# First batch of an attention and gated feed-forward kernel: pooled products written four times into the banks of the banded ones

## The chip, the cores and the metric

The kernel runs on one core of a Trainium2 chip. The metric is the time of one execution on the device in microseconds (us), as the median of several runs. Engines are named as the profile names them: PE is TensorE (PEld its weight loads), DVE VectorE, ACT ScalarE, POOL GpSimd, SP SyncE, which issues the DMAs.

## The reference, cut to what matters

```python
q, k, v: (8, 8, 576, 64) float32; w_in: (512, 2048), w_out: (2048, 512)
# attention, per batch and head
q_d, k_d, v_d = means of four neighbouring rows of q, k, v
out_d   = softmax(q_d k_d^T / 8) v_d                 # 144 rows
mask    = |i - j| < 4
out_loc = softmax(where(mask, q k^T / 8, -1e9)) v    # 576 rows
x = repeat(out_d, 4 rows each) + out_loc             # -> (4608, 512)
# gated feed-forward
h = x @ w_in
out = (h * clip(h + 3, 0, 6) / 6) @ w_out
```

## The kernel before, in words

Work is planned as a list of operations with engines, costs and due times; `Plan.emit` orders them by list scheduling into one queue for each engine, and every queue runs strictly in that order. What an operation may wait for is therefore decided by its place in the queue and by its semaphores.

**Attention.** A unit is one batch and two heads (`plan_unit`, 4 units for each of 8 batches); two units are a duo (`plan_duo`). A unit computes the pooled products (rows of q and k summed in fours, `scores_d`, softmax, `trans_d`, `evict_d`, `pv_d`) and the banded ones (`scores`, ten windows of 64 rows, softmax, `trans`, `evict`, `pv`). v's rows are summed in fours by `sum4` (L361 to L370), by DVE or POOL. For the first batch (b = 0) and the second (`ALONE`) everything is turned by TensorE. `mean` (L551) scales the pooled result and takes it from PSUM to SBUF as `od`, and `add` (L614) adds `od`, each column four times, to the banded result in PSUM and writes x^T to SBUF: for the first batch as 288 + 224 columns in `x0` and 64 in `tail`.

**Feed-forward.** Tokens go in 12 parts (`PART`: 512, 256, then ten of 384). `plan_split` makes x^T's two parts (`hi`, a rounded copy, and `lo`, the rest). For each part and each of 16 blocks f of the hidden width, `gemm1` makes 12 matmuls (L860), `relu`, `gate`, `hi` and `lo` follow on ACT, DVE and POOL, and `gemm2` makes 3 matmuls for each 128 tokens (L910). `plan_store` evicts (L830, L832) and stores (L836).

**Weights.** They arrive as 64-bit floats, 512 KB a block, 32 blocks, and are made into two parts each by `plan_weight`: `rebias` and `low` on ACT (L172, L176, L190), `bits` twice on DVE (L181, L185), `hi` on ACT (L195), `lo` on DVE or POOL (L199).

`busy` (L943) fills expected gaps of TensorE with matmuls whose result nobody reads.

```python
nc.vector.tensor_tensor(x.rearrange("e (q r) -> e q r", r=4), px[...],
    od[:, lo // 4:hi // 4].unsqueeze(2).broadcast_to([P, (hi - lo) // 4, 4]), op=ALU.add)
```

Of the kernel before, what the change touches and what calls it, by code (L numbers as in the profile page):

```python
# [56 lines left out]
def tile_local_down_attention_moe(ctx, tc, q_all, k_all, v_all, _qk_loc, _v_loc, w_in, w_out, ident_d, _mask_d, out):  # L57
# [34 lines left out]
    def buf(key, holder, shape):  # L92
# [34 lines left out]
    head = const.tile([NAR, 2], F32, name="head")  # L127

# [23 lines left out]
    raw_t, zf_t, win, wout = {}, {}, {}, {}  # L152
    w_half, w_hi, w_done = {}, {}, {}

    def plan_weight(n, kind, f, after, gate):
        key = kind, f
        words = {}

        def load():
            raw_t[key] = wts.tile([P, 1024], I32, name=f"raw{kind}{f}", tag=f"w{kind}{f}")  # L160
            nc.sync.dma_start(raw_t[key], (w_in if kind == "i" else w_out)[f].bitcast(I32))
            w = raw_t[key].rearrange("p (n t) -> p n t", t=2)
            words["low"], words["high"] = w[:, :, 0], w[:, :, 1]

        by_bank = n < EARLY_BLOCKS and n % BY_BANK[1] < BY_BANK[0]
        zs = "zs0" if n < EARLY_Z[0] else "zs1" if n < EARLY_Z[1] else "zs"

        def rebias():

            if by_bank:  # L170
                zf_t[key] = bank(place[0], key)
                nc.scalar.activation(zf_t[key], words["high"].bitcast(F32), AF.Copy, scale=2.0 ** -112)  # L172
            else:
                zf_t[key] = buf(zs, key, [P, 512])
                high = words["high"].bitcast(F32)
                nc.scalar.activation(high, high, AF.Copy, scale=2.0 ** -112)  # L176

        def bits(i):
            z, high = zf_t[key].bitcast(I32), words["high"]
            if i == 0:  # L180
                nc.vector.scalar_tensor_tensor(  # L181
                    out=z, in0=z if by_bank else high, scalar=3, in1=words["low"],
                    op0=ALU.logical_shift_left, op1=ALU.bitwise_or)
            else:
                nc.vector.scalar_tensor_tensor(  # L185
                    out=z, in0=high, scalar=-0x80000000, in1=z, op0=ALU.bitwise_and, op1=ALU.bitwise_or)

        def low():

            nc.scalar.activation(words["low"], words["low"].bitcast(U32), AF.Copy, scale=2.0 ** -29, bias=-0.5)  # L190

        def hi():
            w = wts.tile([P, 2, 512], F32R, name=f"w{kind}{f}", tag=f"w{kind}{f}")
            (win if kind == "i" else wout)[f] = w
            nc.scalar.copy(w[:, 0], zf_t[key])  # L195

        def lo(eng):
            w = (win if kind == "i" else wout)[f]
            eng.tensor_tensor(w[:, 1], zf_t[key], w[:, 0].bitcast(F32), op=ALU.subtract)  # L199

        ld = op("SP", 0.5, load, list(after) + ([w_hi[gate]] if gate else []), size=dma(P, 4096))
        place = "zf0" if by_bank else zs, key
        a = op("ACT", 0.68, rebias, [ld], take=[place], lag=LAGW)
        c = op("ACT", 0.68, low, [ld], lag=LAGW)
        b = op("DVE", 0.75, partial(bits, 0), [a, c], lock=not by_bank)
        d = op("DVE", 0.75, partial(bits, 1), [b], lock=not by_bank)
        e = w_hi[key] = op("ACT", 0.6, hi, [d])
        if by_bank:
            w_done[key] = op("DVE", 0.72, partial(lo, nc.vector), [e], free=[place])
        else:  # L210
            w_done[key] = op(on("lo", 1.0), 0, lo, [e], free=[place], lock=True)


    xt = {}
# [72 lines left out]
    def plan_unit(b, d, u, row0, k0, kv, PS, duo, evicts, users, masked, early_user, due):  # L287
# [7 lines left out]


# [49 lines left out]
        def ld4(g):  # L346
            if b == 0 and "raw4" not in st:
                st["raw4"] = buf("raw4", ("v", un), [P, 2, 4, ROW])
            raw = st["raw4"][:, g] if b == 0 else buf("raw" + k0, ("v", un, g), [P, 4, ROW])
            if g == 0:  # L350
                nc.sync.dma_start(raw, src(v_all, row0, [[4 * ROW, P], [1, 4 * ROW]]))
            else:
                n = 1 if alone else 2
                raw = raw[:n * KR]
                for h in range(n):
                    nc.sync.dma_start(
                        raw[h * KR:(h + 1) * KR], src(v_all, row0 + 4 * P, [[4 * ROW, KR], [1, 4 * ROW]]))
            st["raw", g] = raw

        def sum4(g, eng):  # L360
            if "vd" not in st:  # L361
                st["vd"] = buf("vd" + k0, un, [P, 2, ROW])
            raw = st["raw", g]
# [6 lines left out]
            if g and not alone:  # L370
# [3 lines left out]
                eng.memset(st["vd"][NAR:D, 1], 0.0)  # L374

# [5 lines left out]
        for g in range(2):  # L381
            rk = ("raw4", ("v", un)) if b == 0 else ("raw" + k0, ("v", un, g))
            l = op("SP", 0.5, partial(ld4, g), take=[rk], size=dma((P, KR if alone else NAR)[g], 2048), nd=1 if alone else 1 + g)
            if b == 0:
                loads.append(l)
            sums.append(early_user(op(
                on("sum4", 1.0), 0, partial(sum4, g), [l], take=[("vd" + k0, un)], free=[rk])))
# [42 lines left out]
        def weigh(x, p, m, s):  # L430
# [5 lines left out]
            nc.scalar.activation(s, s, AF.Copy, bias=1e-9)  # L436
# [19 lines left out]
        def norm(eng, x, s):  # L456
            eng.tensor_tensor(x, x, s.unsqueeze(2).broadcast_to(list(x.shape)), op=ALU.mult)  # L457
# [952 lines left out]
```

## Time and profile before

| | |
|---|---|
| median of 3 runs | 957.76 us (956.91 to 960.08) |
| profiled execution, its own time | 956.95 us |
| its span, first to last instruction | 954.8 us |
| PE busy | 931.0 us, 98% of the span |
| DVE, ACT, POOL busy | 573.0, 368.2, 279.3 us |
| first matmul of the feed-forward starts at | 40.26 us |
| DMA | 93.53 MB, 98 GB/s in the mean |

How to read it: a share of busy time is a mean over stages. The feed-forward's matmuls of 10 of the 12 parts run back to back; what is not spent there lies in the first third and in the last microseconds. A matmul of float32 operands leaves two records in the trace (an operation of 4 matmuls is x8), a transpose and a matmul of the rounded type one.

### The profile page before, as it was taken

Reading aid. Unit: us, or ns where it says so; the run is one execution under the profiler, and the core shown is the slowest. Engines: PE = TensorE matmul, PEld = TensorE weight load, DVE = VectorE, ACT = ScalarE, POOL = GpSimd, SP = SyncE. Lnnn points to the kernel's source line nnn. Section 1 sums busy time; section 2 is a strip of 40 time slices with the busy share of each in tenths; the row PEclk is TensorE's granted clock in tenths of the full one; section 3 lists DMA queues with packets and bytes.
Section 4 is the critical chain, followed back from the end, with each engine's and each line's share of the span. In section 5 each row is a group of like instructions: output and inputs, shape, how many; then the busy total and the mean of one; then the engine's idle time right before and its main releaser. Section 6 shows DMA issues by size and latency. Waiting matters only on the chain.

```text
span 954.8 us, 19793 instructions
## 1 busy us (share of the span) xinstructions
PE 931.0 (98%) x7498; PEld 805.4 (84%) x7498; DVE 573.0 (60%) x1096; ACT 368.2 (39%) x915; POOL 279.3 (29%) x371
## 2 busy tenths in 40 slices
PE   7979999999999999999999999999999999999996
PEld 4667777888888888888988888888988888998995
DVE  6989887677656566657356667556656463222322
ACT  4787654434334324333233323423433332322321
POOL 5945434244434334323023342214113110000000
PEclk9999999999999999999999999999999999999999
DMA  7996435356665554555424464644514420100101
GB/s 213 265 307 128 126 107 102 81 113 131 120 130 113 118 112 97 102 87 112 94 62 83 102 117 83 128 90 99 117 27 92 94 61 1 34 1 1 34 1 33
DMA packets 311376, 93.53 MB, mean 98 GB/s; under 512 B 251377, under 2 KB 297329, under 8 KB 311281
## 3 DMA queue, kind: packets, MB, share of 16 engines
q1 hardware_dynamic: 311280, 92.27, 43.2%
q8 instruction: 59, 0.97, 0.4%
q14 instruction: 37, 0.29, 0.1%
HBM read 69.60 MB, written 22.61 MB: 97 GB/s over the span
## 4 chain that ended last, share of the span: by engine, by line
PE 88%; DMA 3%; SPq 2%; DVE 2%; POOL 2%; ACT 1%; issue 1%; DVEq 0%; POOLq 0%
PE h L860 40%; PE o L910 40%; PE a L612 2%; PE a L572 2%; PE a L413 1%; PE a L535 1%; PE a L910 1%; DMA early<-in_v_dram 1%; DMA rawo<-in_w_out_dram 1%; DMA rawi<-in_w_in_dram 1%; SPq L300 1%; POOL early L368 1%; SPq L252 0%; SPq L487 0%; DVE arena L870 0%
## 5 line engine op out<-in xcount | busy, mean ns | idle before, releaser
L860 PE MATMUL h<-rounded,wi 128*128 128x384 f32 (+2 forms) x2240 | 433.2, 336 | 5.0 <-ACT wi L195 3.7
L910 PE MATMUL o<-wo,rounded 128*128 128x512 f32 x1680 | 429.1, 396 | 1.0 <-POOL rounded L878 0.9
L860 PEld LDWEIGHTS h<-rounded,wi 128*128 128x128 f32 x2240 | 389.8, 188 | 28.5 <-ACT wi L195 4.5
L910 PEld LDWEIGHTS o<-wo,rounded 128*128 128x128 f32 x1680 | 308.1, 188 | 62.4 <-issue 4.6
L870 DVE SCALAR_TENSOR_TENSOR arena<-arena,h 128x384 f32<-128x384 f32 (+2 forms) x192 | 105.0, 547 | 175.0 <-ACT arena L866 174.5
L866 ACT ACTIVATE arena<-h 128x384 f32<-128x384 f32 (+2 forms) x192 | 94.1, 490 | 285.5 <-PE h L860 279.9
L874 ACT CAST rounded<-arena 128x384 fp32r<-128x384 f32 (+2 forms) x192 | 98.4, 513 | 145.9 <-DVE arena L870 107.8
L878 DVE TENSOR_TENSOR rounded<-arena,rounded 128x384 fp32r<-128x384 f32 (+2 forms) x154 | 87.1, 567 | 103.0 <-PE o L910 77.0
L878 POOL TENSOR_TENSOR rounded<-arena,rounded 128x384 fp32r<-128x384 f32 (+2 forms) x38 | 42.8, 1126 | 213.2 <-PE o L910 137.9
L442 POOL TENSOR_TENSOR arena<-arena 128x640 f32<-128x640 f32 x23 | 29.0, 1263 | 71.1 <-DVE arena L439 70.9
L307 DVE STREAM_TRANSPOSE arena<-arena 128x576 f32<-128x576 f32 x56 | 42.8, 767 | 11.7 <-DMA arena<-in_q_dram 6.8
L787 POOL TENSOR_TENSOR rounded<-arena,rounded 128x768 fp32r<-128x768 f32 (+2 forms) x6 | 8.8, 1472 | 94.9 <-DVE rounded L121 82.3
L428 ACT ACTIVATE arena<-arena 128x2 f32<-128x2 f32 (+2 forms) x54 | 10.6, 197 | 63.4 <-DVE arena L439 63.4
L520 DVE STREAM_TRANSPOSE arena<-arena 128x640 f32<-128x640 f32 x24 | 20.2, 841 | 22.8 <-DMA arena<-pl 22.6
L434 ACT ACTIVATE arena<-a,arena 128x144 f32<-128x144 f32 x84 | 31.5, 379 | 1.8
L457 DVE TENSOR_TENSOR arena<-arena 128x432 f32<-128x432 f32 (+1 forms) x38 | 31.5, 830 | 1.0
L501 DVE STREAM_TRANSPOSE arena<-arena 128x384 f32<-128x384 f32 (+1 forms) x48 | 21.6, 463 | 15.6 <-DMA arena<-pd 15.3
L368 POOL TENSOR_TENSOR arena<-arena 128x256 f32<-128x256 f32 (+2 forms) x37 | 29.2, 789 | 4.6 <-DMA arena<-in_v_dram 3.3
L322 POOL TENSOR_TENSOR arena<-arena 128x144 f32<-128x144 f32 x46 | 29.1, 633 | 3.6
L572 PE MATMUL a<-arena 64*64 64x64 f32 x1220 | 29.6, 224 | 0.0
L320 POOL TENSOR_TENSOR arena<-arena 128x144 f32<-128x144 f32 x23 | 11.8, 515 | 60.7 <-DMA arena<-in_k_dram 16.6
L439 DVE TENSOR_REDUCE arena<-a 128x2 f32<-128x288 f32 (+3 forms) x63 | 25.1, 406 | 3.9 <-PE a L572 2.0
(185 smaller groups left out, 853.7 us busy)
## 6 DMA issues: line engine op xcount, KB each, us to landing
rawi<-in_w_in_dram SPq DMA_DIRECT2D x16, 512.0 KB
rawo<-in_w_out_dram SPq DMA_DIRECT2D x16, 512.0 KB
arena<-in_q_dram SPq DMA_DIRECT2D x112, 72.0 KB
arena<-in_k_dram SPq DMA_DIRECT2D x112, 72.0 KB
pl<-arena SPq DMA_DIRECT2D x24, 320.0 KB
arena<-pl SPq DMA_DIRECT2D x96, 80.0 KB
arena<-in_v_dram SPq DMA_DIRECT2D x28, 256.0 KB
out_dram<-arena SPq DMA_DIRECT2D x96, 72.0 KB
```

The source lines that it names most:

```text
L307: nc.vector.transpose(out=qk[kind], in_=st["raw", kind].rearrange("p j i -> p (j i)"))
L322: eng.tensor_tensor(t, t, x[:, :, r], op=ALU.add)
L368: eng.tensor_tensor(raw[:, 0:2], raw[:, 0:2], raw[:, 2:4], op=ALU.add)
L434: nc.scalar.activation(p[:, j], x[:, j], AF.Exp, bias=m[:, j:j + 1], scale=1.0 / 128.0, accum_out=s[:, j:j + 1])
L457: eng.tensor_tensor(x, x, s.unsqueeze(2).broadcast_to(list(x.shape)), op=ALU.mult)
L572: nc.tensor.matmul(st["ps", g][half:half + WIN, jj * D:jj * D + WIN], qk_of("q")[hs, k_first:k_first + WIN], qk_of("k")[hs, k_first:k_firs ...
L860: nc.tensor.matmul(st["ps"], win[f][:, wt, kk * P:(kk + 1) * P], xs[part][:, kk], start=(kk == 0 and i == 0), stop=(kk == NK - 1 and i == ...
L866: nc.scalar.activation(st["t"], st["ps"], AF.Relu, bias=3.0)
L870: nc.vector.scalar_tensor_tensor(out=t, in0=t, scalar=6.0, in1=st["ps"], op0=ALU.min, op1=ALU.mult)
L874: nc.scalar.copy(st["gh"], st["t"])
L878: eng.tensor_tensor(st["gl"], st["t"], st["gh"].bitcast(F32), op=ALU.subtract)
L910: nc.tensor.matmul(otile[n, m], gt[:, ms], wout[f][:, wt], start=(f == 0 and i == 0), stop=(f == NF - 1 and i == 2),)
```

## The change

- **Pooled products into the banks of the banded ones** (b = 0, `direct`). `pv_d` no longer writes 144 columns into a bank of its own: it writes each column four times, 72 x 4 = 288 columns, into each of the two banks in which `pv` then adds the banded products (`start=not direct`). `mean`, `add`, `od` and `x0` go. The factor 1/4 goes into the softmax's sum (`weigh`).
- **x^T's parts taken in the banks.** `plan_split` reads part 0 from PSUM, in pieces of 288 and 224 columns; `lo` is DVE's alone there. Only the last 64 columns are copied to SBUF (`tail`).
- **v's sums by TensorE** (b = 0, and the last 16 sums of b = 1): `sum_pe` adds four rows by matmuls with the identity, or with `four`; `evict_v` copies.
- **Weights in pairs**: blocks 6 to 27 of the 32 are worked on two at a time, in tiles of twice the width (`plan_weights`).
- **End by parts**: in the last part the last two blocks f are done tile by tile; each output tile is evicted half by ACT, half by DVE, and stored half by SP's, half by ACT's queue.
- Due times of batches 1 to 3 (`SLACK`, `UNIT_T`), buffers and costs change; for b < 2 the pooled normalization may go to ACT (`normd`).

```diff
+        direct = b == 0
+        def sum_pe(g):
+            st["psv", g] = ps = bank(PS, ("v4", un, g))
+            raw = st["raw", g]
+            if g:
+                nc.tensor.matmul(ps[:KR, :ROW], four[:4 * KR, :KR], raw[:4 * KR, 0], start=True, stop=True)
+            for i in range(0 if g else 4):
+                nc.tensor.matmul(ps[:, :ROW], ident, raw[:, i], start=(i == 0), stop=(i == 3))
...
         def pv_d():
-            st["od"] = buf("od" + k0, un, [P, SD])
-            st["pod"] = ps = bank(PS, ("od", un))[:, :SD]
+            if direct:
+                st["px"] = px[hp] = [bank(PS, ("x", un, g)) for g in range(2)]
...
             for g in range(2):
                 for h in range(2):
                     hs = slice(h * D, (h + 1) * D)
+                    v4, w = st["vd"][:nk[g], g, hs], st["pdt"][:nk[g], g, h]
+                    if not direct:
+                        nc.tensor.matmul(st["pod"][hs], v4, w, start=(g == 0), stop=(g == 1), skip_group_check=True)
+                    for i in range(2 if direct else 0):
+                        q = w[:, i * SD // 2:(i + 1) * SD // 2].unsqueeze(2).broadcast_to([nk[g], SD // 2, 4])
+                        nc.tensor.matmul(
+                            st["px"][i][hs, :HALF].rearrange("p (q r) -> p q r", r=4), v4, q, start=(g == 0), stop=(g == 1),
+                            skip_group_check=True)
...
     def x_of(n, b, k, ks, s0, cnt):
         if b:
             return xt[b][:, k:k + ks, s0:s0 + cnt]
-        return xt[0, k].unsqueeze(1) if n == 0 else xt[0, "tail"][:, k:k + ks]
+        return px[k][s0 // HALF][:, :cnt].unsqueeze(1) if n == 0 else xt[0, "tail"][:, k:k + ks]
...
+            e = [op("ACT", 0.37, partial(ev_half, 0, nc.scalar), [ready], take=[("obz", (n, m))], free=[frees])]
+            e.append(op("DVE", 0.37, partial(ev_half, 1, nc.vector), [ready] + e, take=[("obz", (n, m))], free=[frees]))
+            op("SP", 1.2, partial(store_half, 0, nc.sync), e, free=[("obz", (n, m))], size=dma(P, 1024), nd=3)
+            op("ACT", 1.0, partial(store_half, 1, nc.scalar), e, free=[("obz", (n, m))])
...
-UNIT_T, EARLY, SLACK = (4.0, 22.0, 30.0), 0.7, 28.0
+UNIT_T, EARLY, SLACK = (4.0, 22.0, 20.0, 30.0), 0.7, (4.0, 40.0, -5.0, 28.0)
...
+PAIRED = 6, 28
-EARLY_BLOCKS = 10
-EARLY_Z = 14, 21
+EARLY_Z = 14, 28
```

**Where instructions move.** PE's queue, before, from the turning of the last unit's banded weights to the first matmuls of the feed-forward (L595 `trans`, L546 `pv_d`, L860 `gemm1`; `o_`, `a_`, `h_` are PSUM banks):

```order
L595 MATMUL o_668<-ident,early 128x128 x3
L595 MATMUL o_672<-ident,early 128x128 x2
L546 MATMUL a_677<-early 64x144 x4
L860 MATMUL h_688<-rounded,wi_598 128x512
L860 MATMUL h_688<-lo,wi_598 128x512
L860 MATMUL h_688<-rounded,wi_598 128x512 x2
```

PE's queue with the change, where the first `pv_d` stands (L393 and L391 `sum_pe`, L501 `trans_d`, L638 `trans`, L589 `pv_d`, whose eight matmuls alternate between two banks):

```order
L393 MATMUL a_460<-early,ident 128x128 x4
L391 MATMUL a_474<-early,four 16x128
L638 MATMUL o_477<-ident,arena 128x128 x3
L393 MATMUL o_484<-early,ident 128x128 x4
L501 MATMUL a_497<-ident,early 128x128 x3
L501 MATMUL a_506<-ident,early 16x128 x3
L391 MATMUL o_513<-early,four 16x128
...
L638 MATMUL o_530<-ident,arena 128x128 x2
L589 MATMUL o_536<-arena 64x288
L589 MATMUL a_537<-arena 64x288
```

v's sums are now matmuls between the turnings, and `pv_d` has 8 matmuls of 288 columns where it had 4 of 144. Behind the first unit's banded scores and ahead of the first `gemm1`, PE's queue has 11 matmuls of `busy`, where it had 22.

DVE's queue, before, around the last block of `w_in` (rawi_1323, wi_1854; used by h_1867, part 0's last block f; L870 is the gate, of f = 13 and 14 here):

```order
L870 SCALAR_TENSOR_TENSOR arena<-arena,h_1707 128x512
L366 TENSOR_REDUCE arena<-arena 128x128
L629 TENSOR_TENSOR arena<-a_1798,arena 128x288
L629 TENSOR_TENSOR arena<-a_1799,arena 128x288
L181 SCALAR_TENSOR_TENSOR arena<-rawi_1323 128x512
L181 SCALAR_TENSOR_TENSOR arena<-rawo_1616 128x512
L185 SCALAR_TENSOR_TENSOR arena<-rawi_1323,arena 128x512
L185 SCALAR_TENSOR_TENSOR arena<-rawo_1616,arena 128x512
L878 TENSOR_TENSOR rounded<-arena,rounded 128x512
L199 TENSOR_TENSOR wi_1854<-arena,wi_1854 128x512
L307 STREAM_TRANSPOSE arena<-arena 128x576
L870 SCALAR_TENSOR_TENSOR arena<-arena,h_1774 128x512
```

DVE's queue with the change around the same block, which is now the first half of the pair rawp_1253 (L944 is the gate, of f = 11 and f = 12 here; L185 and L189 are `bits`):

```order
L944 SCALAR_TENSOR_TENSOR arena<-arena,h_1505 128x512
L189 SCALAR_TENSOR_TENSOR early<-rawp_1248,early 128x1024
L185 SCALAR_TENSOR_TENSOR early<-rawp_1253 128x1024
L485 RECIPROCAL arena<-arena 128x3
L189 SCALAR_TENSOR_TENSOR early<-rawp_1253,early 128x1024
L205 TENSOR_TENSOR wp_1576<-early,wp_1576 128x2x512
L470 TENSOR_REDUCE arena<-a_1584 128x5
L470 TENSOR_REDUCE arena<-a_1585 128x5
L473 TENSOR_TENSOR arena<-a_1584,arena 128x5x64
L473 TENSOR_TENSOR arena<-a_1585,arena 128x5x64
L944 SCALAR_TENSOR_TENSOR arena<-arena,h_1562 128x512
```

The bits of the block that f = 15 reads stood between the gates of f = 13 and 14, and now stand between those of f = 11 and 12.

ACT's queue with the change, its last rows (L899 evicts half a tile, L905 stores; before, no store stood on ACT and its last row was a cast):

```order
L899 ACTIVATE arena<-o_9289 128x256
L905 DMA out_dram<-arena 36x512
L905 DMA out_dram<-arena 32x512
L899 ACTIVATE arena<-o_9303 128x256
L899 ACTIVATE arena<-o_9327 128x256
L905 DMA out_dram<-arena 36x512 x4
```

Seven of the last 13 stores stay with SP, six go to ACT's queue; of those the last four stand behind the last tile's eviction.

## Rows read from the trace of the kernel before

**Rows 1.** Windows: stretch, busy us (x instructions) by engine, granted clock, DMA share, GB/s.

```profile
13.20:66.70 53.50, 43.92 (x551) 30.34 (x549) 44.73 (x96) 41.58 (x106) 36.67 (x52) 0.94 0.87 256
66.70:300.00 233.30, 229.67 (x2002) 191.66 (x1999) 177.06 (x329) 114.22 (x284) 104.09 (x124) 1.00 0.55 121
300.00:939.00 639.00, 639.00 (x4784) 570.21 (x4783) 338.85 (x647) 207.52 (x520) 135.20 (x187) 1.00 0.36 75
```

**Rows 2.** Timeline of PE, 9 to 67 us: start, us, instruction [idle before <- releaser].

```profile
9.12 0.43 PE L564 MATMUL a<-maskb,identb 128*128 128x320 bf16 x2
10.46 0.95 PE L399 MATMUL a<-early,arena 64*64 64x144 f32 x12
11.35 0.44 PE L564 MATMUL o<-maskb,identb 128*128 128x320 bf16 x2
...
15.08 0.49 PE L265 MATMUL a<-ident,rows 128*128 128x128 f32 x3
15.41 0.49 PE L265 MATMUL o<-ident,rows 128*128 128x128 f32 x3
...
28.20 1.03 PE L943 MATMUL h<-identb 128*128 128x512 bf16 x4
...
36.48 0.84 PE L466 MATMUL o<-ident,early 128*128 128x128 f32 x6
37.25 0.86 PE L546 MATMUL a<-early 128*64 128x144 f32 x8
38.04 0.81 PE L612 MATMUL a<-arena,early 64*64 64x60 f32 x40
38.78 0.76 PE L595 MATMUL o<-ident,early 128*128 128x128 f32 x5
39.47 0.86 PE L546 MATMUL a<-early 128*64 128x144 f32 x8
...
66.68 0.50 PE L860 MATMUL h<-rounded,wi 128*128 128x512 f32 x1
```

**Rows 3.** Groups of PE's instructions by line and form, 39 to 66.6 us.

```profile
L860 PE MATMUL h<-rounded,wi 128*128 128x512 f32 x32 | 12.4, 446 | 2.9 <-ACT wi L195 2.9
L860 PE MATMUL h<-lo,wi 128*128 128x512 f32 x16 | 7.2, 450 | 0.8 <-POOL lo L787 0.8
L910 PE MATMUL o<-wo,rounded 128*128 128x512 f32 x3 | 0.8, 390 | 0.0
```

**Rows 4.** The chain that ended last, 95 to 112 us: start, us, what.

```profile
99.41 2.72 PE h L860 x12
```

**Rows 5.** Timeline of SP's queue, 10 to 36 us.

```profile
13.16 0.60 SPq L340 DMA_DIRECT2D early<-in_v_dram  x1
...
23.68 6.01 SPq L300 DMA_DIRECT2D arena<-in_q_dram  x4
```

**Rows 6.** Waits of SP's queue over the span: total us, times, longest.

```profile
SPq L340 <- DMA rows<-in_k_dram: 2.1, 1, 2.1
```

**Rows 7.** Waits of PE, 146 to 155 us: total us, times, longest.

```profile
PE h L860 <- ACT wi L195: 0.7, 1, 0.7
PE h L860 <- DVE wi L199: 0.5, 1, 0.5
```

**Rows 8.** Timeline of all engines, 936 to 955 us.

```profile
939.06 8.36 PE L910 MATMUL o<-wo,rounded 128*128 128x512 f32 x36
...
946.10 1.37 DVE L832 TENSOR_SCALAR arena<-o 128x512 f32<-128x512 f32 x2 [4.13 <-PE o L910]
946.82 5.61 SPq L836 DMA_DIRECT2D out_dram<-arena  x13
949.87 0.69 DVE L832 TENSOR_SCALAR arena<-o 128x512 f32<-128x512 f32 x1 [2.39 <-DMA out_dram<-arena]
```

**Rows 9.** Timeline of PE, 32.4 to 32.75 us.

```profile
32.50 0.27 PE L612 MATMUL a<-early 64*64 64x60 f32 x2
32.53 0.27 PE L612 MATMUL o<-early 64*64 64x57 f32 x2
```

More of the change, by code (lines that the diff above doesn't have):

```diff
@@ L143, in make_identb @@
         nc.vector.tensor_copy(identb, ident)
+        nc.vector.tensor_reduce(out=four, in_=ident.rearrange("p (c r) -> p c r", r=4), op=ALU.add, axis=AX.X)
     def make_mask():
@@ L148, in make_mask @@
             nc.vector.tensor_reduce(out=head[:, h:h + 1], in_=ident[:NAR, h * KR:(h + 1) * KR], op=ALU.add, axis=AX.X)
[L152 to L156, printed above, removed]
-        words = {}
[L159 to L166, printed above, removed]
-        def rebias():
[L170 to L176, printed above, removed]
+    win, wout = {}, {}
@@ L197, in lo @@
+            for i, (kind, f) in enumerate(keys):
+                (win if kind == "i" else wout)[f] = w[:, i]
+            nc.scalar.copy(w[:, :, 0], words["z"])
         def lo(eng):
[L198 to L207, printed above, removed]
+            w = words["w"]
+            eng.tensor_tensor(w[:, :, 1], words["z"], w[:, :, 0].bitcast(F32), op=ALU.subtract)
+        cols = 512 * nk
+        lds = [op("SP", 0.5, partial(load, i), list(after) + ([w_hi[gate]] if gate else []), size=dma(P, 4096))
+               for i in range(nk)]
@@ L208, in plan_weight @@
+        a = op("ACT", 0.2 + cols / 1070, rebias, lds, take=[place], lag=LAGW)
+        c = op("ACT", 0.2 + cols / 1070, low, lds, lag=LAGW)
+        b = op("DVE", 0.2 + cols / 930, partial(bits, 0), [a, c], lock=not by_bank)
+        d = op("DVE", 0.2 + cols / 930, partial(bits, 1), [b], lock=not by_bank)
+        e = op("ACT", 0.13 + cols / 1090, hi, [d])
         if by_bank:
-            w_done[key] = op("DVE", 0.72, partial(lo, nc.vector), [e], free=[place])
+            g = op("DVE", 0.72, partial(lo, nc.vector), [e], free=[place])
@@ L603, in pv @@
         def pv():
-            st["px"] = [bank(PS, ("x", un, g)) for g in range(2)]
+            if not direct:
+                st["px"] = [bank(PS, ("x", un, g)) for g in range(2)]
             for jj in range(5):
@@ L713, in plan_unit @@
             bk = (PS, ("od", un))
[L714 to L715 removed]
+            if direct:
+                a = early_user(op("PE", 2.0, pv_d, evs_d + sums, take=[(PS, ("x", un, g)) for g in range(2)], free=[tk_d, ("vd" + k0, un)],
+                                  lag=LAGT, rec=16))
+            else:
+                a = op("PE", 0.64, pv_d, evs_d + sums, take=[bk, ok], free=[tk_d, ("vd" + k0, un)], lag=LAGT, rec=8)
+                od = op("ACT", 0.29, mean, [a], free=[bk])
+            done_d = [a]
             t = []
@@ L734, in plan_unit @@
             od = op("DVE", 0.31, mean_too, [od], free=[bks[1]])
-        adds = []
-        for g in range(2):
-            adds.append(early_user(op("DVE", 0.45, partial(add, g), [a, od], free=[bks[g]], dl=due)))
-        plan.free_after(ok, adds)
+        if direct:
+            op(on("ev", S - TOK0), 0, tail, [a], take=xbs, free=[bks[1]])
+            adds = [a]
+        else:
+            adds = [op("DVE", 0.45, partial(add, g), [a, od], free=[bks[g]], dl=due) for g in range(2)]
+            plan.free_after(ok, adds)
         for kind in "qk":
@@ L1015 @@
     "norm": {"DVE": (0.15, 1 / 960), "POOL": (0.2, 1 / 420)},
+    "normd": {"DVE": (0.15, 1 / 960), "POOL": (0.2, 1 / 420), "ACT": (1.0, 0.0)},
     "xhi": {"ACT": (0.15, 1 / 1100), "DVE": (0.1, 1 / 960)},
```

197 lines of the change are left out of this document (129 added, 68 removed).

## The prediction

> **What bounds the kernel now.** I read the windows first [rows 1]: from 300 to 939 us PE is busy without a gap, and from 66.7 to 300 it is idle for 3.6 of 233.3 us. The feed-forward's matmuls are the bound there, and their number does not change. So time can come from three places only: the 53.5 us from 13.2 to 66.7, in which PE is busy for 43.9 and idle for 9.6 at a granted clock of 0.94 [rows 1]; the 3.6 us; and the end, where PE has nothing to do from 947.4 (939.06 + 8.36) [rows 8] to the end of the span at 954.8. Against that stand the operations that the change adds to PE's queue. The timeline of PE [rows 2] then gives the price of each kind of operation, the groups [rows 3] the count of feed-forward matmuls done by 66.7 us.
>
> All sums stand against the profiled execution, 956.95 us; the median of the runs shown is 0.8 above it. A measurement of this kernel can tell about 0.3%, 2.9 us, from no change.
>
> **Part 1, the first batch.** I count PE's queue of the changed kernel as a plain sum, without waits, from one fixed point to another. The start is 13.2 us: SP's queue shows k's second block of rows landing then [rows 5, 6], the loads ahead of it are the same, and with the change the turning of those rows stands ahead of all pooled scores. The end is the place that the kernel before reaches at 66.68 [rows 2]: banded products of the second batch's first unit done, 48 + 3 feed-forward matmuls done [rows 3]. Up to there the changed queue holds, each price being the distance between starts [rows 2]:
>
> - 3 turnings of rows, 15.41 - 15.08 = 0.33: 1.0
> - 5 pooled scores, 11.35 - 10.46 = 0.89: 4.5
> - 4 banded scores, 10.46 - 9.12 = 1.34: 5.4
> - 5 pairs of `trans_d`, 37.25 - 36.48 = 0.77: 3.9
> - 5 `trans`, 39.47 - 38.78 = 0.69: 3.5
> - 5 `pv`, 38.78 - 38.04 = 0.74: 3.7
> - 1 `pv_d` of the second batch, 38.04 - 37.25 = 0.79: 0.8
> - 4 new `pv_d`, 2.6 each (below): 10.4
> - 4 large sums of v, 8 records of 128 columns at 0.33 / 3 = 0.11: 3.5; 5 small ones, 2 records each: 1.1
> - 11 matmuls of `busy`, 1.03 / 4: 2.8
> - 51 feed-forward matmuls, 2.72 / 12 = 0.227 [rows 4]: 11.6
>
> Sum 52.2, so the place is reached at 65.4: **1.3 us sooner**. Put differently, the new sums and the wider `pv_d` add 11.8 us to PE and 11 fewer matmuls of `busy` take 2.8 away; the idle 9.6 us and the slower clock pay for it.
>
> The new `pv_d` has no row. The old one makes 8 records in four steps of 0.79 / 4 = 0.198 us, since its two heads use different columns of the array and start together; 144 more columns at 0.33 / 384 = 0.86 ns each add 0.124 us a step, so 0.322, and there are now eight steps: 2.6 us. The lower end takes the pooled scores' step, 0.89 / 6 = 0.148: (0.148 + 0.124) x 8 = 2.2. The upper end is no overlap of the heads, sixteen steps: 5.2. I take 2.6, from the row of the same operation; the ends give -1.6 and +10.4 us.
>
> What is hidden: DVE loses 12 `add`s and two sums and gains eight `lo`s from PSUM; it was busy for 44.7 of the 53.5 us [rows 1], so it stays below PE's sum, with little to spare. POOL (36.7 of 53.5) loses four `lo`s and the sums of v, which it had ahead of the normalizations. ACT (41.6) loses `mean` and gains copies of 128 columns. I cost these three at nothing; if DVE's waits come on top, that is a rival. Loads: the v windows now go out ahead of the rows to be summed, and only one weight block instead of four ahead of the second batch's q and k, whose first four loads took SP 6.0 us [rows 5]; they land sooner, the next weights later.
>
> **Part 2, 66.7 to 300 us.** The last small sums of v of the second batch's other three units are 3 x 0.22 = 0.7 us more on PE, in a stretch without slack: **+0.7**. In the kernel before, PE waits 1.2 us for the last block of w_in near 150 us [rows 7]; its bits now stand two gates sooner on DVE, so I let that wait go: **-1.2**. The other 2.4 us of idle time I leave. Pairs save some fixed time on ACT and DVE, off the path: nothing, as long as PE is fed. Bounds: all 3.6 us go, or new due times bring as much again.
>
> **Part 3, the end.** Before: PE ends at 947.4, but the third tile's eviction waits until 949.87 for the first tile's stores, ends at 950.56, its four stores go out until 946.82 + 5.61 = 952.43 (0.47 each), and the last lands by 954.8, 2.4 later [rows 8]. With the change each tile has its own buffer, and tiles 1 and 2 are finished 2.7 and 1.4 us ahead of tile 3 (6 matmuls each, 0.227). For tile 3: 0.2 us to start, 0.4 for ACT's half (half of 0.69 and a fixed part); then ACT's queue sends four stores, 1.9 us (the DVE half, 0.5 later, is hidden behind the first two), and 2.4 to land: 947.4 + 4.9 = 952.3 against 954.8, **-2.5**. If a store from ACT's queue takes twice as long to send, the gain is 0.6; if the halves and landing are brisk, 3.2.
>
> **Sum:** -1.3 + 0.7 - 1.2 - 2.5 = -4.3; 956.95 - 4.3 = 952.6, and **952.5 us** is the forecast.
>
> **The rivals.**
> *More of the idle time goes.* `pv_d` at 2.2 (-1.6) and the remaining 2.4 us of idle time gone: 952.6 - 4.0 = 948.6. For it: POOL's chain of sums and normalizations, the longest wait of the first 40 us, is gone. Against: due times were moved, and PE's waits are not named by them.
> *Waits stay.* PE's queue of the first batch is not the bound; DVE's and ACT's are, since each stands in order behind the second batch's q and k, whose turning now sits ahead of the first batch's last sums. If a third of the 9.6 us of idle time remains, +3.2: 955.8, no change. For it: DVE at 44.7 of 53.5.
> *Heads overlap only in part.* In program order the new `pv_d` makes both halves of head 0 ahead of head 1. If matmuls start strictly in that order, a group needs three places and adjoining groups share one: five places of two matmuls where I count four, 2.6 x 5/4 = 3.25, and 4 x 0.65 = +2.6: 955.2, at the edge of no change. The Trainium skill, "TensorE: Matmul & The Clock Gate", Part 3, "The mechanism", states that matmuls are strictly first in, first out in start and end. The trace speaks against it for these float32 matmuls: of the banded products, bank a has two records from 32.50 and bank o two from 32.53 [rows 9], while program order and two records a matmul would put four of bank a first; so records of later matmuls overtake. That lowers its chance, and does not exclude it.
> *Heads do not overlap* (the slower side). Two same-head matmuls in a row leave the array's other columns empty, sixteen steps: 5.2 us a unit, 4 x 2.6 = +10.4: 963. It decides from about 4.6 us a unit (4 x 2.0 = 8 us more reach 960.6). For it: in the trace such matmuls always alternate heads, so no row shows overlap without that. Against: the overtaking just named.
>
> **How the numbers follow.** The sum as forecast (949.5 to 954.9) 0.46; more idle time gone 0.16; waits stay 0.16; partial overlap 0.12, half of it within 0.3%; no overlap, or a like cost in due times, 0.10. Faster by over 0.3% (below 954.9): 0.46 + 0.16 + 0.06 = 0.68; within: 0.16 + 0.06 = 0.22; slower (above 960.6): 0.10. The range leaves out most of the slowest case and the tail of the best: **946.5 to 959.0**; with the forecast's own 949.5 to 955.
>
> **What would show each step.** Right: PE between 13 and 65 us with less than 3 us of idle time; four `pv_d` of 2.2 to 2.8 us each; the first batch's place (51 feed-forward matmuls, second batch's first banded product) near 65.4; no wait for w_in near 150; last instruction some 5 us behind PE's last matmul. Wrong: `pv_d` of 3.2 us or more; PE waiting for DVE's `lo` (L837) or for weights between 40 and 60 us; a new wait of over 1 us at the borders of parts 1 to 3; stores from ACT's queue of 0.9 us each.

## The result, and the profile after

Measured in the same session, the changed kernel took 949.51 us in the median of three runs (948.73 to 951.57) and the kernel before 958.25; the ratio is 0.9912 (95% interval 0.989 to 0.9934). The forecast was 952.5 us, range 946.5 to 959.0, "faster" at 0.68: sign and range hold, and the gain is larger than forecast. The execution of the changed kernel that was profiled first ran throughout at a lower granted clock (0.68 in the mean, 1266.92 us) and is left out of the median, so the profile shown below is of a later one, 949.98 us, its span 948.1. The six runs of that later session have the median 949.98 against 958.3 for 17 runs of the kernel before (0.991, 0.9888 to 0.9933).

The windows of the changed kernel, in the columns of [rows 1]: stretch, busy us (x instructions) of PE, PEld, DVE, ACT, POOL, then granted clock, DMA share, GB/s.

```profile
13.20:66.70 53.50, 52.07 (x670) 35.27 (x670) 46.23 (x94) 41.42 (x107) 26.09 (x33) 1.00 0.89 254
66.70:300.00 233.30, 232.79 (x2028) 196.54 (x2027) 175.95 (x311) 115.96 (x274) 96.27 (x107) 1.00 0.55 123
300.00:939.00 639.00, 639.00 (x4778) 569.46 (x4777) 337.98 (x644) 206.02 (x518) 134.57 (x184) 1.00 0.36 74
```

PE's idle time falls from 9.6 to 1.4 us in the first stretch and from 3.6 to 0.5 in the second; the clock, 0.94 there before, is 1.00. POOL's busy time falls from 36.7 to 26.1 us.

PE's waits of the kernel before: the three longest from 13.2 to 66.7 us, and behind the dots all from 66.7 to 300 (total us, times, longest):

```profile
PE a L466 <- POOL early L457: 3.0, 1, 3.0
PE h L860 <- ACT wi L195: 2.9, 1, 2.9
PE a L546 <- ACT arena L119: 2.1, 2, 1.7
...
PE o L910 <- POOL rounded L878: 0.9, 1, 0.9
PE h L860 <- ACT wi L195: 0.7, 1, 0.7
PE h L860 <- DVE rounded L787: 0.7, 1, 0.7
PE h L860 <- DVE wi L199: 0.5, 1, 0.5
PE a L612 <- DVE arena L121: 0.4, 1, 0.4
```

The same of the changed kernel; in the first stretch only a wait for k's rows is left out, which ends as the stretch begins, and behind the dots stands all of the second:

```profile
PE o L638 <- ACT arena L120: 0.6, 1, 0.6
PE o L638 <- DVE arena L122: 0.6, 1, 0.6
PE h L934 <- DVE arena L944: 0.3, 1, 0.3
...
PE h L934 <- DVE arena L944: 0.5, 1, 0.5
```

POOL's normalization, the copy ahead of `pv_d` and every wait for weights are gone. Left are two copies of 128-column blocks ahead of `trans` and two waits for a gate.

PE's timeline of the changed kernel (start, us, instruction): prices of the new operations and the place to which the forecast counted.

```profile
28.67 1.06 PE L393 MATMUL o<-early,ident 128*128 128x128 f32 x8
29.56 0.82 PE L501 MATMUL a<-ident,early 128*128 128x128 f32 x6
30.31 0.39 PE L391 MATMUL o<-early,four 64*16 64x128 f32 x2
30.63 1.04 PE L1035 MATMUL h<-identb 128*128 128x512 bf16 x4
...
41.38 2.32 PE L589 MATMUL o<-early 128*64 128x288 f32 x16
43.63 0.50 PE L934 MATMUL h<-rounded,wp 128*128 128x512 f32 x1
...
65.77 0.84 PE L984 MATMUL o<-wp,rounded 128*128 128x512 f32 x3
66.54 0.39 PE L391 MATMUL a<-arena,four 64*16 64x128 f32 x2
```

A new `pv_d` takes 43.63 - 41.38 = 2.25 us here (so do the first and the last of the four; the second took 2.60, rows below), a large sum of v 29.56 - 28.67 = 0.89, a small one 30.63 - 30.31 = 0.32. The 51st feed-forward matmul is done at 66.54 us, where the kernel before was at 66.68 [rows 2].

The end of the changed kernel, all engines, as [rows 8]:

```profile
934.88 8.36 PE L984 MATMUL o<-wp,rounded 128*128 128x512 f32 x36
...
943.28 0.38 ACT L899 ACTIVATE arena<-o 128x256 f32<-128x256 f32 x1 [0.39 <-PE o L984]
943.37 2.25 SPq L905 DMA_DIRECT2D out_dram<-arena  x5
943.38 1.63 ACTq L905 DMA_DIRECT2D out_dram<-arena  x4
```

PE ends at 943.24 (934.88 + 8.36) instead of 947.4, and the span ends at 948.1: 4.9 us of tail instead of 7.4. So the span's 6.7 us (954.8 - 948.1) come from three places: 0.1 up to the place, 4.0 between the place and PE's end (947.43 - 66.68 = 880.75 before, 943.24 - 66.54 = 876.70 now), 2.5 behind PE's end.

### The profile page after: what moved, and what is told of

It reads as the page before. It is cut to its first block, busy times and chain, and to the rows that moved or that the text cites. A ratio compares the mean times of both kernels' runs of the same rounds, so it can differ in the third digit from the quotient of the medians.

```text
span 1265.1 us, 19848 instructions
## 1 busy us (share of the span) xinstructions
PE 1257.1 (99%) x7567; PEld 928.4 (73%) x7567; DVE 569.2 (45%) x1070; ACT 371.3 (29%) x906; POOL 254.1 (20%) x334
## 3 DMA queue, kind: packets, MB, share of 16 engines
q1 hardware_dynamic: 311376, 91.83, 32.4%
## 4 chain that ended last, share of the span: by engine, by line
PE 99%; DMA 0%; SPq 0%; DVE 0%; ACT 0%; issue 0%
PE h L934 43%; PE o L984 42%; PE a L656 2%; PE a L615 2%; PE a L442 1%; PE a L570 1%; PE a L984 1%; PE o L589 1%; PE a L428 1%; PE a L501 0%; PE h L1035 0%; PE a L638 0%; DMA arena<-in_k_dram 0%; PE o L274 0%; PE a L586 0%; PE o L638 0%
## 5 line engine op out<-in xcount | busy, mean ns | idle before, releaser
L934 PE MATMUL h<-rounded,wp 128*128 128x384 f32 (+2 forms) x2240 | 571.8, 414 | 0.0
L984 PE MATMUL o<-wp,rounded 128*128 128x512 f32 x1680 | 568.0, 494 | 0.0
L934 PEld LDWEIGHTS h<-rounded,wp 128*128 128x128 f32 x2240 | 449.7, 208 | 103.9 <-issue 14.7
L984 PEld LDWEIGHTS o<-wp,rounded 128*128 128x128 f32 x1680 | 339.7, 206 | 151.3 <-issue 35.2
L944 DVE SCALAR_TENSOR_TENSOR arena<-arena,h 128x384 f32<-128x384 f32 (+2 forms) x192 | 105.8, 551 | 347.0 <-ACT arena L940 346.5
L837 POOL TENSOR_TENSOR rounded<-arena,rounded 128x768 fp32r<-128x768 f32 (+2 forms) x10 | 13.0, 1315 | 123.9 <-DVE rounded L122 115.0
L615 PEld LDWEIGHTS a<-arena 64*64 64x64 f32 x1220 | 33.8, 150 | 2.5 <-issue 1.8
L376 DVE TENSOR_REDUCE arena<-arena 128x128 f32<-128x512 f32 (+1 forms) x20 | 21.0, 1056 | 29.6 <-PE a L570 22.5
L331 POOL TENSOR_TENSOR arena<-arena 128x144 f32<-128x144 f32 x22 | 9.9, 448 | 119.7 <-PE a L442 57.6
L470 DVE TENSOR_REDUCE arena<-a 128x1 f32<-128x144 f32 (+2 forms) x65 | 26.2, 411 | 16.3 <-PE a L615 7.5
L656 PEld LDWEIGHTS a<-arena 64*64 64x64 f32 x1120 | 23.6, 164 | 13.0 <-issue 11.2
L934 PE MATMUL h<-lo,wp 128*128 128x512 f32 x64 | 32.4, 506 | 0.0
L205 POOL TENSOR_TENSOR wp<-early,wp 128x1024 fp32r<-128x1024 f32 (+1 forms) x9 | 19.3, 2153 | 54.4 <-ACT wp L201 43.2
```

The lines of the kernel that those rows point to most:

```text
L470: nc.vector.tensor_reduce(out=m, in_=x, op=ALU.max, axis=AX.X)
L615: nc.tensor.matmul(st["ps", g][half:half + WIN, jj * D:jj * D + WIN], qk_of("q")[hs, k_first:k_first + WIN], qk_of("k")[hs, k_first:k_firs ...
L656: nc.tensor.matmul(st["px"][g][h * D:(h + 1) * D, at + lo:at + hi], st["v"][ks, jj, h * D:(h + 1) * D], st["pt"][ks, jj, half + lo:half + ...
L934: nc.tensor.matmul(st["ps"], win[f][:, wt, kk * P:(kk + 1) * P], xs[part][:, kk], start=(kk == 0 and i == 0), stop=(kk == NK - 1 and i == ...
L944: nc.vector.scalar_tensor_tensor(out=t, in0=t, scalar=6.0, in1=st["ps"], op0=ALU.min, op1=ALU.mult)
L984: nc.tensor.matmul(otile[n, m], gt[:, ms], wout[f][:, wt], start=(f == 0 and i == 0), stop=(f == NF - 1 and i == 2),)
```

## The experiments

Times are medians. Each ratio compares with the kernel before, run on the same chip beside it (its medians there were 958.3 to 959.35 us); 949.98 us is the changed kernel's own, from the session of `a_same`, and differences from it in microseconds are across chips for `e_unpaired` and all that follow.

**The changed kernel again** (`a_same`), for the profile above.

> The changed kernel unaltered, for a clean profile beside the kernel before on the same chip. The first result gave about 8.4 us (0.9%) against a forecast of 4.3 (from the profiled execution) to 5.7 us (from the median). Theory 1 (each term about as forecast, one mis-sized): the place of 51 feed-forward matmuls and the second batch's first banded product at 62 to 65.4 us instead of 66.68, pv_d 2.2 to 2.6 us each, the last instruction 4 to 5 us behind PE's last matmul instead of 7.4. Theory 2 (the gain lies in the end alone): the place at 66 to 67, the last instruction less than 3 us behind PE's last matmul. Theory 3 (the middle, 66.7 to 300 us, by pairs and due times): the place near 65.4, but idle time of PE between there and 300 us below 1 us instead of 3.6, and PE's work there shorter by over 2 us.

The place at 66.54 speaks against a shorter first batch, the tail of 4.9 against the end alone; with 0.5 us of idle time behind 66.7 the third theory is the nearest, though the place did not come near 65.4 as it wanted.

**Order of the heads in `pv_d`** (`b_order`).

```diff
-                for h in range(2):
+                for i, h in ((0, 0), (0, 1), (1, 0), (1, 1)) if direct else ((0, 0), (0, 1)):
...
-                    for i in range(2 if direct else 0):
+                    if direct:
```

> The new pv_d's eight matmuls in an order that alternates the two heads (column halves of the array) instead of making both banks of one head first. If matmuls of the two heads overlap only where they stand next to each other (the rival of partial overlap), this gains: three steps a group instead of two, so up to 4 units x 0.65 = 2.6 us sooner than the changed kernel, and pv_d's time from start to start falls from about 3.2 to 2.6 us. If records of later matmuls overtake (the forecast's reason), nothing changes: within 0.5 us, pv_d the same in both. If heads did not overlap at all in the changed kernel, it gains 8 us or more.

950.82 us (ratio 0.9918, 0.9895 to 0.9941), no difference from the changed kernel. PE's timeline of this kernel has the same operation in the same time, 43.69 - 41.46 = 2.23 us:

```profile
41.46 2.31 PE L589 MATMUL o<-early 128*64 128x288 f32 x16
43.69 0.50 PE L934 MATMUL h<-rounded,wp 128*128 128x512 f32 x1
```

And the changed kernel's first two units, each matmul leaving two records. Program order in the first is bank o, then bank a of head 0, then bank o, then bank a of head 1; in the second it begins with bank a:

```profile
31.82 0.71 PE L589 MATMUL o<-arena 128*64 128x288 f32 x4
32.35 0.66 PE L589 MATMUL a<-arena 128*64 128x288 f32 x4
...
34.07 0.82 PE L589 MATMUL a<-early 128*64 128x288 f32 x3
...
36.67 0.55 PE L638 MATMUL o<-ident,early 128*128 128x128 f32 x3
```

All four records of bank o, head 1's two among them, start ahead of the first of bank a, which is head 0's. The records overtake, as the forecast read from the banded products [rows 9], and both rivals on the heads fall. In the second unit the records do not pair up so from the start (three of bank a stand first), and it took 36.67 - 34.07 = 2.60 us. With alternating heads the second unit took 36.68 - 34.33 = 2.35 us, and the others 2.23 or 2.24.

**The old end on the changed kernel** (`c_end_old`).

```diff
-        if n == len(PART) - 1:
+        if False:
...
-            if n == len(PART) - 1 and f == NF - 2:
+            if False:
```

(the condition for `last_two` likewise)

> The changed kernel with the end of the kernel before: three tiles in rotating buffers, evicted whole by DVE and stored by SP's queue alone, last blocks f not sorted by tiles. The forecast's third term says 2.5 us slower than the changed kernel (bounds 0.6 to 3.2), the last instruction again 7.4 us behind PE's last matmul. If the end carries most of the 8.4 us (theory 2): 5 us or more slower. If it is hidden by something else: the same within 0.5 us.

952.96 us (ratio 0.9942, 0.9919 to 0.9964): 3.0 slower than the changed kernel, where 2.5 were expected. Its end by the timeline:

```profile
939.74 3.11 PE L984 MATMUL o<-wp,rounded 128*128 128x512 f32 x13
...
945.23 0.69 DVE L884 TENSOR_SCALAR arena<-o 128x512 f32<-128x512 f32 x1 [2.33 <-DMA out_dram<-arena]
```

PE ends at 942.85 and the span at 950.3, 7.5 us later: the third tile's eviction again waits for the first tile's stores.

**The new end on the kernel before** (`d_end_only`): the same code of `plan_store` and `last_two` put into it.

> The kernel before with the new end alone (own buffer for each of the three last tiles, halves evicted by ACT and DVE, stores from SP's and ACT's queues, last two blocks f tile by tile). Forecast's third term: 2.5 us faster than the kernel before (bounds 0.6 to 3.2), and nothing changes ahead of 900 us. Theory 2 (the end alone): 6 to 8 us faster. If the terms add, the gain here and the loss of the kernel with the old end agree to within 0.7 us.

957.49 us against 958.3 (ratio 0.9985, 0.9968 to 1.0002): by the runs, whose own spread (953.28 to 959.46) is wider than the term, the gain is 0.8 us, and neither nothing nor the 2.5 forecast is excluded. Its profile shows the term: PE ends at 945.90 and the span at 951.2, 5.3 us of tail instead of 7.4. By the tails the gain here (2.1) and the loss with the old end (7.5 - 4.9 = 2.6) agree within the 0.7 us expected; by the medians (0.8 and 3.0) they do not. Up to 900 us this kernel's engines run the same instructions in the same order as the kernel before, and yet its PE is idle for 6.65 us from 13.2 to 66.7 where [rows 1] have 9.6:

```profile
13.20:66.70 53.50, 46.85 (x557) 32.39 (x556) 46.78 (x99) 43.07 (x108) 38.20 (x54) 0.90 0.92 264
```

So the first batch of the kernel before varies by this much between two executions: less idle time, and a lower clock (0.90 for 0.94).

**Single weights** (`e_unpaired`), **old due times** (`f_due_old`).

```diff
-PAIRED = 6, 28
+PAIRED = 6, 6
```

```diff
-UNIT_T, EARLY, SLACK = (4.0, 22.0, 20.0, 30.0), 0.7, (4.0, 40.0, -5.0, 28.0)
+UNIT_T, EARLY, SLACK = (4.0, 22.0, 30.0, 30.0), 0.7, (4.0, 24.0, 28.0, 28.0)
```

> The changed kernel with every weight block worked on singly (no pairs). In the clean profile of the changed kernel PE's end comes 4.2 us sooner than before, and only 0.2 of that is reached by 66.5 us; the rest is won up to 300 us, where idle time falls from 3.6 to 0.5 us. Theory P (pairs win the middle: fewer and longer operations on ACT and DVE, weights done sooner): idle time of PE from 66.7 to 300 back at 2.5 us or more, waits for weights named, time 2 to 4 us longer than the changed kernel. Theory D (the due times win it): idle time there stays below 1.2 us, the time within 1 us of the changed kernel. The forecast counted pairs as nothing.

> The changed kernel with the due times of before for batches 1 to 3. Theory D: idle time of PE from 66.7 to 300 back at 2.5 us or more, with waits for attention's or the gate's operands (the five waits of before were 0.4 to 0.9 us each), 2 to 4 us longer than the changed kernel. Theory P: within 1 us of the changed kernel. Either way the place of 51 feed-forward matmuls and the second batch's first banded product may move, as the second batch's units stand elsewhere.

957.62 us (0.9994, 0.9977 to 1.0011) and 963.73 us (1.0046, 1.0025 to 1.0067): 7.6 and 13.8 slower than the changed kernel, where 2 to 4 were expected of each. Neither theory excludes the other: both bring idle time back in the middle. PE's waits from 66.7 to 300 us with single weights (idle time 4.2 us):

```profile
PE a L656 <- DMA arena<-in_v_dram: 2.4, 1, 2.4
PE a L656 <- DVE arena L122: 0.7, 1, 0.7
...
PE o L984 <- DVE wp L205: 0.5, 1, 0.5
```

then the windows with the old due times, and behind the dots the longest waits of the second window:

```profile
13.20:66.70 53.50, 53.47 (x634) 37.17 (x635) 46.64 (x97) 43.84 (x106) 26.45 (x33) 0.97 0.91 271
66.70:300.00 233.30, 224.03 (x1943) 186.21 (x1942) 168.29 (x297) 106.90 (x247) 81.83 (x95) 0.97 0.52 115
...
PE h L934 <- POOL rounded L837: 3.1, 2, 2.7
PE a L638 <- DVE arena L492: 1.8, 1, 1.8
PE a L501 <- DVE arena L473: 1.5, 1, 1.5
```

With single weights most of the new idle time is not a wait for weights (0.5 us) but for a load of v (2.4 us) and for two copies (0.7 each). With the old due times the first stretch has no idle time at all, and the 51st feed-forward matmul is done at 61.8 us; but the other half of the forecast's place, the second batch's first banded product, starts at 71.6 us (62.2 in the changed kernel). 9.3 us of idle time come later, for the second batch's attention (the softmax ahead of L501 and L638) and for the split of x^T's part 2 (L837), whose tokens are the second batch's. The clock is 0.97 in both windows, so the loss is not idle time alone.

**v's sums by DVE and POOL** (`g_sum4`, with the loads and sums of v's rows that this needs) and **pooled products in their own bank** (`h_no_direct`: `direct = False`, with `add`, `x0` and the split from SBUF put back).

```diff
...
-            if b == 0 or alone and g:
+            if False:
                 bk = PS, ("v4", un, g)
...
```

```diff
-        direct = b == 0
+        direct = False
...
-        return px[k][s0 // HALF][:, :cnt].unsqueeze(1) if n == 0 else xt[0, "tail"][:, k:k + ks]
+        return xt[0, k].unsqueeze(1) if n == 0 else xt[0, "tail"][:, k:k + ks]
...
```

> The changed kernel with v's rows summed by DVE and POOL as before, TensorE's sums taken out. By the forecast's sum the matmuls of v's sums cost PE 4.6 us up to the place (4 at 0.88, 5 at 0.22), 5.8 us by the clean profile. If the waits that they take away are as long (the kernel before had 3.0 us for POOL's normalization and 1.7 for a bank's copy ahead of pv_d), the time stays within 1.5 us and PE is idle for 5 us or more between 13 and 66.7 us. If DVE and POOL still hide the sums now that the pooled products need no adds: 3 us or more faster. If their waits are longer: 2 us or more slower.

> The changed kernel with the first batch's pooled products in a bank of their own again, taken to SBUF by ACT and added by DVE, x^T's parts split from SBUF. PE gets 4 x (2.3 - 0.8) = 6 us less to do by the clean profile; DVE gets twelve adds back and loses eight splits from PSUM. If PE's queue is what bounds the first batch now (idle 1.4 us of 53.5), up to 5 us faster unless filler matmuls take the room; if x^T's path over DVE is what the change shortened, idle time of PE between 40 and 66.7 us comes back (6.1 us before) and the time is within 1.5 us or longer by up to 4.

954.33 us (0.9957, 0.9933 to 0.998) and 959.53 us (1.0017, 0.9998 to 1.0036): 4.4 and 9.6 slower than the changed kernel, the second beyond what was expected. PE's longest waits of the two from 13.2 to 66.7 us, two of `g_sum4` and then one of `h_no_direct`:

```profile
PE a L655 <- DMA arena<-in_v_dram: 2.1, 1, 2.1
PE a L500 <- POOL early L491: 1.7, 1, 1.7
```

```profile
PE a L638 <- DVE arena L673: 2.5, 1, 2.5
```

POOL's normalization is back where POOL sums; DVE's adds (L673) hold up `trans` where they are back. PE is spared some 6 us of work in both kernels, by the counts in the two expectations, and is idle for 5.9 and 9.2 us longer from 13.2 to 300 us (table below).

**No filler** (`i_nobusy`), **new due times alone** (`j_due_before`), **due times halfway** (`l_due_mid`).

```diff
-            o.busy = max(0, int(gap / IDLE[0]))
+            o.busy = 0
```

```diff
-UNIT_T, EARLY, SLACK = (4.0, 22.0, 30.0), 0.7, 28.0
+UNIT_T, EARLY, SLACK = (4.0, 22.0, 20.0, 30.0), 0.7, (4.0, 40.0, -5.0, 28.0)
...
```

```diff
-UNIT_T, EARLY, SLACK = (4.0, 22.0, 20.0, 30.0), 0.7, (4.0, 40.0, -5.0, 28.0)
+UNIT_T, EARLY, SLACK = (4.0, 22.0, 25.0, 30.0), 0.7, (4.0, 32.0, 10.0, 28.0)
```

> The changed kernel without the filler matmuls, whose result nobody reads. They take PE 5.3 us in the clean profile of the changed kernel, 2.7 of them behind 13.2 us. If the filler lies in time in which PE would wait anyway, as planned, and PE's clock does not need it: the same within 0.7 us, idle time up by some 3 to 5 us, granted clock 1.00 throughout. If idle time lowers the clock (before: 3.0 us idle near 17 us and a granted clock of 0.57 in the 4 us behind, another idle stretch at 48 to 52 us and 0.69 behind it): matmuls behind the gaps take longer and the kernel is 1 to 5 us slower. If the filler stood in the way of real work: up to 2.7 us faster.

> The kernel before with the new due times of batches 1 to 3 and nothing else. The changed kernel with the old ones was 14 us slower, with 9.3 us of idle time between 66.7 and 300 us. If the due times are worth that by themselves: 5 us or more faster than before, idle time from 66.7 to 300 below 1 us. If they only fit the changed kernel (its first batch leaves DVE and POOL room for the second batch's early units): no faster or slower than before, and idle time of PE between 13 and 66.7 us grows beyond 9.6 us, since the second batch now stands in the way of the first.

> The changed kernel with due times about halfway between the old and the new ones (second batch's units less early, third's less late). With the old ones the first batch's place came at 61.8 us without any idle time, but 9.3 us of idle time came back later; with the new ones 66.5 and 0.5. If idle time is a smooth trade between the two stretches: the place at 63 to 65 us, idle time later 3 to 5 us, the time 2 to 8 us longer. If the waits fall where single operations collide: anything from 3 us faster to 5 us slower, with waits not seen in either. A version that beats both would show less than 2 us of idle time behind 66.7 and a place ahead of 66 us.

Without filler 950.02 us (0.9913, 0.9893 to 0.9933), the same as with it; idle time rises by 2.2 us, 3 to 5 were expected. The new due times in the kernel before give 960.57 us (1.0024, 1.0008 to 1.0039), slower by about 2, so they gain nothing by themselves; the first stretch's idle time did not grow as expected (8.6 us, 9.6 before), but its clock is 0.90 and 4.6 us of idle time follow. Halfway: 959.23 us (1.0009, 0.9989 to 1.0028), 9.2 slower than the changed kernel, beyond the 2 to 8 expected; the 51st feed-forward matmul is done at 61.8 us, but the second batch's first banded product, due by then too, starts only at 77.1, so the place does not come at 63 to 65 as expected, and 6.2 us of idle time come later (3 to 5 expected). No version beats the changed kernel.

**A nudge** (`n_nudge`), one due time moved by 2 us:

```diff
-UNIT_T, EARLY, SLACK = (4.0, 22.0, 20.0, 30.0), 0.7, (4.0, 40.0, -5.0, 28.0)
+UNIT_T, EARLY, SLACK = (4.0, 22.0, 20.0, 30.0), 0.7, (4.0, 38.0, -5.0, 28.0)
```

> A control for the experiments that undo one part: the changed kernel with one due time moved by 2 us (the second batch's, 40 to 38), all parts in place, so that the planner writes another order with the same operations. The four undone parts cost 4 to 14 us each, 35 us in sum, where the whole change gives 8.3. If those costs are mostly the price of an order that was not tuned for the kernel at hand: this control loses 2 us or more as well, with idle time of PE up by as much. If they are the price of the parts themselves: within 1 us of the changed kernel (949 to 951.5 us), idle time of PE behind 13.2 us below 3 us.

950.62 us (0.9919, 0.9898 to 0.994): this other order of the same operations costs nothing that can be measured. The due times halfway are the same operations in another order too, and cost 9.2 us. PE's idle time and the granted clock in all profiles, idle time being the length of the window less PE's busy time:

| kernel | idle, 13.2 to 66.7 us | idle, 66.7 to 300 us | clock in the two | median us |
|---|---|---|---|---|
| before | 9.6 | 3.6 | 0.94, 1.00 | 958.3 |
| changed | 1.4 | 0.5 | 1.00, 1.00 | 949.98 |
| no filler | 2.6 | 1.5 | 1.00, 1.00 | 950.02 |
| nudge | 0.6 | 2.2 | 1.00, 1.00 | 950.62 |
| order of heads | 1.7 | 1.7 | 1.00, 1.00 | 950.82 |
| old end | 1.5 | 0.5 | 1.00, 1.00 | 952.96 |
| sums by DVE, POOL | 4.6 | 3.3 | 0.97, 1.00 | 954.33 |
| before, new end | 6.7 | 3.8 | 0.90, 1.00 | 957.49 |
| single weights | 2.8 | 4.2 | 1.00, 0.99 | 957.62 |
| due times halfway | 0.5 | 6.2 | 1.00, 0.98 | 959.23 |
| own bank | 5.8 | 5.3 | 0.90, 0.98 | 959.53 |
| before, new due times | 8.6 | 4.6 | 0.90, 1.00 | 960.57 |
| old due times | 0.0 | 9.3 | 0.97, 0.97 | 963.73 |

Where a part is undone, 5 to 9 us of idle time come back somewhere, not always where the part stands. The four parts undone cost 4.4, 7.6, 9.6 and 13.8 us, 35 in sum, of a whole that gives 8.3: they are not shares that add. How much of each is the price of the part, and how much that of an order planned with due times that were chosen with the part in place, no run separates.

## Why the prediction was right, and where it was not

- **The end: right, -2.5 forecast, -2.5 measured** in the profiles, 3.0 by the runs of the kernel with the old end. ACT's last four stores take 1.63 / 4 = 0.41 us each (0.47 forecast). The path is not the one named: ACT's queue is done at 945.0 (943.38 + 1.63), SP's, with five of the last nine stores, at 945.6, and 2.5 us later the last has landed. That the sum held all the same is luck: the two queues differ by only 0.6 us.
- **The first batch: -1.3 forecast, -0.1 measured.** PE's work was counted well: from 13.2 to 66.54 there are 53.3 us, less 1.4 idle, 51.9 of work where 52.2 were counted (three of the new `pv_d` 0.35 cheaper than their 2.6, a small sum 0.1 dearer than its 0.22). What failed is the sentence "I cost these three at nothing": copies by ACT and DVE and a gate still hold PE up for 1.4 us. That is the "waits stay" rival at less than half its price. The statement that idle time and the slower clock pay for the new work is shown: 8.2 us of idle time went, and the clock is 1.00.
- **The middle: -0.5 forecast, -4.0 measured.** This is the term that failed, in "The other 2.4 us of idle time I leave" and "Pairs ...: nothing". Of 3.6 us of idle time 3.1 went, where 1.2 were let go (the wait near 150 us is gone, as forecast). The three small sums behind the place cost 3 x 0.32 = 1.0, not 0.7. That makes -2.1, and even the bound named in Part 2 (all 3.6 us go) gives only -2.9. The rest is in how a wait was priced, at the idle time shown. Behind the place PE's records of the two kernels are the same in kind and number, but for the six of the small sums, and from 66.7 to 300 us the clock is 1.00 in both. The starts of the records around the wait near 150 us, in the kernel before, show what a wait takes:

```profile
148.78 0.84 PE L910 MATMUL a<-wo,rounded 128*128 128x512 f32 x3
150.34 0.50 PE L860 MATMUL h<-rounded,wi 128*128 128x512 f32 x1 [0.72 <-ACT wi L195]
150.68 0.40 PE L860 MATMUL h<-lo,wi 128*128 128x512 f32 x1
```

Three matmuls at 0.23 us would have let the next start at 149.47; it starts 0.87 us later, where 0.72 of idle time is shown, as that is counted from the end that the profile gives the matmul before. The step behind the wait is 0.34 instead of 0.23 us. Taken this way, as an estimate from the starts, the waits from 66.7 to 300 us took some 5.6 us in the kernel before, and 0.8 in the changed one: 4.8 less, and with 1.0 for the sums 3.8 of the 4.0. The rival "more of the idle time goes" had the loss of waits as its mechanism, and its 948.6 lies 1.4 below the profiled execution. With single weights idle time comes back in the middle, though only 0.5 us of it as a wait for weights; which of the five old waits which part took is open, as every undone part brought back other waits than the old ones.
- **Heads.** The rival of partial overlap wanted 3.25 us a unit; it took 2.25 in the order as written, once 2.60, and 2.24 to 2.35 with alternating heads. The Trainium skill, "TensorE: Matmul & The Clock Gate", Part 3, "The mechanism", states that matmuls are strictly first in, first out in start and end; the records of this case do not agree with it (bank o's four from 31.82, bank a's four from 32.35 us).
- **The reference.** The forecast stood against the profiled 956.95 us, the sum gave 952.6, and the changed kernel's profile took 949.98: 2.6 off. The middle gave 3.5 more and the first batch 1.2 less, so two errors partly cancel, and 0.3 lies outside the spans. The 8.3 us between medians hold 1.35 more, because the profiled execution of the kernel before was among its quicker ones: its medians in five sessions are 958.25 to 959.35, and its runs spread over more than 6 us. The changed kernel's spread over 3.

## What to carry to other kernels

Where one engine's queue is full to the end of the kernel, the time is its work, its idle time wherever it lies, and the tail: list all three over the whole span, and forecast the idle time of every stretch, not of the one that was edited alone. Price a wait by the starts of the instructions around it, since the idle time shown can leave part of it out. The added matmuls of the first batch, 11.8 us by the forecast's count, cost no time here because 8.2 us of idle time, half the filler and the slower clock went there. A first stretch without any idle time (old due times) belonged to the slowest kernel of all: it did 51 feed-forward matmuls 4.8 us sooner by leaving the second batch's attention for later, and PE was idle for 9.3 us there. Undoing one part of a jointly tuned change measures what the rest loses without it, not the part's share. A control that only reorders helps to judge that, but one is not enough: the nudge cost nothing, the due times halfway 9.2 us.

## What the runs showed of the hardware that was not expected

Idle time on PE can be paid more than once. Windows of the kernel before, ahead of and in two slow stretches (columns of [rows 1]):

```profile
16.00:20.00 4.00, 1.74 (x10) 0.64 (x7) 1.23 (x4) 3.92 (x12) 3.55 (x8) 1.00 0.67 178
20.00:24.00 4.00, 3.29 (x49) 2.41 (x50) 2.61 (x4) 0.44 (x2) 3.69 (x8) 0.57 0.81 208
...
48.00:52.00 4.00, 1.14 (x3) 0.77 (x4) 3.98 (x9) 3.97 (x12) 0.00 (x0) 0.88 0.76 116
52.00:56.00 4.00, 4.00 (x13) 3.13 (x13) 3.72 (x7) 2.17 (x4) 3.41 (x3) 0.69 0.74 176
```

Behind these two idle stretches, of 2.98 and 2.94 us, the granted clock fell, to 0.57 and 0.69 as means over 4 us, so for much of that time it stood at the lower of its two levels, 1.2 of 2.4 GHz. Seven matmuls of `gemm1` behind the second, from 51.32 to 54.32 us, took 0.43 us each from start to start, where later ones took 0.23: 1.4 us on top of the wait. The idle stretch of 1.74 us ahead of 61.31 was not followed by a fall (1.00 from 60 to 64 us). The 32 matmuls of `gemm1` with x^T's first part took 446 ns each in the kernel before [rows 3] and 418 in the changed one, the 16 with its second part 450 and 393:

```profile
L934 PE MATMUL h<-rounded,wp 128*128 128x512 f32 x32 | 12.1, 418 | 0.3 <-DVE arena L944 0.3
L934 PE MATMUL h<-lo,wp 128*128 128x512 f32 x16 | 6.3, 393 | 0.0
```

Idle time is not needed for a fall. With the old due times PE was idle for no more than 0.03 us at a time from 20 to 40 us; from 31.00 it ran two new `pv_d`, whose matmuls are 64 columns wide, half of them with 16 rows (the forms 128*64 and 16*64), and at 35.66 the clock fell all the same:

```profile
32.00:35.66 3.66, 3.66 (x31) 1.58 (x32) 2.40 (x5) 3.31 (x7) 1.03 (x1) 1.00 0.70 93
35.66:39.07 3.41, 3.41 (x48) 2.31 (x49) 2.95 (x8) 1.14 (x4) 0.79 (x2) 0.50 0.86 307
```

In the changed kernel the same two operations stand one behind the other (31.82 to 36.67 us), and no fall followed. Why one fell and the other did not, no run here shows.

The filler, which was there to bridge idle gaps, is of no measurable use to the changed kernel. Without it the windows have a clock of 1.00 as well:

```profile
13.20:66.70 53.50, 50.92 (x668) 34.93 (x668) 47.41 (x95) 42.66 (x110) 26.03 (x33) 1.00 0.91 256
```

The other thing not expected is how little the order of the heads matters to matmuls of two halves of the array: eight matmuls in either order took 2.23 and 2.25 us, and 2.60 at most.
